# Attention values with weights block-diagonal over two heads, and one more weight unit kept on the chip

## The chip, the cores and the metric

The kernel runs on one core of a Trainium2 chip. A core has five engines that run their own instruction streams: TensorE (PE, matmuls and weight loads), VectorE (DVE), ScalarE (ACT), GpSimd (POOL) and SyncE (SP, which only issues transfers here). SBUF is the on-chip memory of 128 partitions, PSUM the accumulator memory of 128 partitions with eight banks, and 16 DMA engines move data between memory and SBUF. The metric is the time of one execution on the device in microseconds, taken as the median of the runs.

## The reference

The output is the sum of the input, a memory-augmented attention over the normalized input, and a feed-forward block. The attention is a recurrence over 64 segments of 32 tokens: eight memory rows come out of each segment and go into the next.

```python
def _A_ref(x, mem0, Wq, Wk, Wv, Wo, seg_len):       # x (1, 2048, 1024), 32 heads of 128
    mask = (idx[:, None] < M) | (idx[:, None] >= idx[None, :])      # M = 8 memory rows, L = 40
    mem = mem0
    for s in range(n_seg):                                          # 64 segments
        h = jnp.concatenate([mem, x[:, s * seg_len:(s + 1) * seg_len]], axis=1)   # 40 rows
        q, k, v = (einsum('btd,dhe->bhte', h, W) for W in (Wq, Wk, Wv))
        scores = jnp.where(mask, einsum('bhqe,bhke->bhqk', q, k) * scale, -1e9)
        o = einsum('bhqk,bhke->bhqe', softmax(scores), v)
        o = einsum('bhte,hed->btd', o, Wo)
        mem = o[:, :M]
        outs.append(o[:, M:])
    return jnp.concatenate(outs, axis=1)

xn = _layernorm(x)
return x + _A_ref(xn, ...) + (gelu(xn @ w1 + b1) @ w2 + b2)
```

All weights are bfloat16. Wq, Wk, Wv and Wo hold 4 x 8 MB. They don't all fit in SBUF, and every segment needs all of them.

## The kernel before

The feed-forward block and the normalization run first, up to about 370 us. Then comes a loop over the 64 segments. The weights are cut into 64 units of 128 x 2048 elements (512 KB): 16 each of K, Q, V and O, each of K, Q and V in two half passes (u = 0 and 1: heads 0 to 15 and 16 to 31) of eight units. 46 units stay in SBUF. 18 are brought anew in every segment into a ring of six slots; of these one is copied from PSUM, where it is kept in two of eight banks (IN_PSUM), and one (HALF) has half of it in a third bank and the other half in a place of its own in SBUF (half_home), so 16 whole units per segment come from memory.

```python
PLACED = "S....S.." "..S....S" "...S...S" "...S...S" "....S..." ".S.S..S." ".S..S..S" "..S..S.S"   # S: streamed
IN_PSUM = [unit for unit in ORDER if IS_STREAMED[unit]][3]
HALF = [unit for unit in ORDER[48:] if IS_STREAMED[unit]][3]

def start_stream(slot):                    # called whenever a streamed unit has been used
    n = starts.popleft()
    unit, t = streams[n], slab(slot)
    if unit in kept_in:
        for c0, bank in kept_in[unit]:
            nc.vector.tensor_copy(out=t[:, c0:c0 + 1024], in_=bank)        # L228
    elif unit in copies:
        nc.sync.dma_start(out=t[:, :], in_=copies[unit])                   # L230
```

A unit of K, Q or V is four matmuls of 512 columns, side by side in four column groups of TensorE (L690). A segment's last eight rows ("left rows") take part in their segment's attention too, but they are projected for four segments together, in one extra product (psL, hrL) in some of the passes. So the four kinds of segment (i4 = 0 to 3) differ in matmul work.

Attention, per half of the heads. The 16 heads lie as four groups c with four heads j each; the keys of head j of a group are on partitions 32j to 32j+31.

```python
def scores(u):                             # mixed: one PSUM bank
    ...                                    # scores of 40 queries x 4 groups into mixed[:, 0:224]
    pr = pr_last[:, 0:224] if u else sp.tile([P, 256], BF16, name="pr", tag="e")[:, 0:224]
    nc.scalar.activation(out=pr, in_=mixed[:, 0:224], func=ACT.Exp, scale=INV_SQRT_DH)
    ...                                    # masks, by min: L811

def sums(u):
    prA, prB = st["pr", u]
    dA = mixed[:, 0:160].rearrange("p (c q) -> p c q", q=40)
    ...                                    # 4 + 4 matmuls with ones, block by block (bd): L819, L825
    nc.scalar.activation(out=dA, in_=dA, func=ACT.Ln)                      # L829
    nc.scalar.activation(out=dA, in_=dA, func=ACT.Exp, scale=-1.0)         # L830
    nc.vector.tensor_tensor(out=prA, in0=prA, in1=dA, op=ALU.mult)         # L831
    nc.vector.tensor_tensor(out=prB4, in0=prB4, in1=ends(dA), op=ALU.mult) # L833

def values(u, r):                          # two heads b of each group, 32 rows each
    V, (prA, prB) = st["V", u], st["pr", u]
    av = [mixed[:, 256:512] if low_bank and b == 0 else new_acc() for b in range(2)]
    oV = [t[:, 0:160].rearrange("p (c q) -> p c q", q=40) for t in av]
    for c in range(4):
        for b in range(2):
            q = slice(64 * r + 32 * b, 64 * r + 32 * b + 32)
            nc.tensor.matmul(oV[b][:, c, :], lhsT=V[q, c * P:(c + 1) * P], rhs=prA[q, c, :], ...)   # L844
        for b in range(2):
            ...                            # the same with the left rows' values VL: L850
    for b, cp in enumerate((nc.scalar.copy, nc.vector.tensor_copy)):
        hs = slice(8 * r + 4 * b, 8 * r + 4 * b + 4)
        cp(out=outs[u][:, hs, NL * slot:NL * slot + 40], in_=oV[b])        # L857
```

The order in a segment: K0, Q0, K1, Q1, V0, V1, O. scores(0) stands after the first unit of Q1, sums(0) after its last; scores(1) after the first unit of V1, values(0, r) and sums(1) further on in V1, values(1, r) in O. In O the first eight units read d_oL (heads of u = 0) and the last eight b_oL (u = 1), 256 columns a matmul (L870). Three PSUM banks serve as accumulators (acc), one holds scores and sums (mixed), one the masks and the queries of left rows (beside), three the kept weights.

At a segment's end the memory rows go through ACT (L954), TensorE (put_mem, L262) and DVE (L266) into hr, which is the left operand of the next segment's products; the residual is added (L969) and the rows go out.

The softmax here doesn't subtract the row's maximum and nothing guards it: scores larger than these inputs give would overflow.

## Time and profile before

| what | value |
|---|---|
| median of three runs | 1960.52 us (1956.52 to 1964.47) |
| span of the profiled execution | 1969.5 us, TensorE clock 0.981 |
| DMA packets, bytes | 219883, 627.06 MB |
| weight transfers in the loop (u<-Wc) | 1024 of 512 KB |
| TensorE's share of the chain that ended last | 69%; DMA 16%, issue 7% |

How to read the views. The page's first part gives busy time, share and instructions of each engine; "PEld" are weight loads, which overlap matmuls. The DMA row gives the share of the 16 DMA engines in each of 40 equal slices, in tenths. A queue's row gives packets, megabytes and the share of the engines' time. A row of a line gives engine, operation, tile, count, shortest, median and longest duration in ns, first and last start in us, and the shape. A row of stretches gives the stretch, its length, busy time and count of PE, PEld, DVE, ACT and POOL, the granted clock, the DMA share and GB/s. A row of waits gives who waited for what, the sum in us, how often, and the longest. In a timeline a bracket is idle time before the instruction and what ended it; "issue" is idle time that no semaphore in the profile ends. Matmuls are pipelined and their ends are modelled, so a busy TensorE is not TensorE at its peak.

### The profile page before, as it was taken

The numbers are of one execution on the slowest core, as the hardware profiler recorded it, in microseconds if no ns is written. First come the engines' busy times: TensorE is split into PE (matmuls) and PEld (weight loads), VectorE is DVE, ScalarE is ACT, GpSimd is POOL, SyncE is SP. The second block draws the span as 40 slices with busy tenths as digits, with TensorE's granted clock in tenths as the row PEclk, the third lists the DMA queues.
The fourth block names the chain that finished last, engine by engine and source line by source line (L and its number), as shares of the span: only waits on it lengthen the run. The fifth ranks groups of instructions, "written<-read, shape, count | busy, mean of one in ns | idle before, by whom it ended". The sixth has DMA issues, their size and how long they took to land.

```text
span 1969.5 us, 77311 instructions
## 1 busy us (share of the span) xinstructions
PE 1774.1 (90%) x34307; PEld 980.5 (50%) x34307; DVE 886.2 (45%) x2280; ACT 599.5 (30%) x1355; POOL 276.2 (14%) x538
## 2 busy tenths in 40 slices
PE   7999999989888989888989889889888889899887
PEld 3444444445545544455555545455446445545544
DVE  6656565414444444344444444344444444444433
ACT  6343434312223323222222222223222222222222
POOL 0000000002421112121112111111111111111111
PEclk9999999999999999999999999999999999999999
DMA  9821212789999999999999999999999999999998
GB/s 331 252 55 43 55 43 54 283 308 341 381 381 375 388 366 365 354 356 364 378 358 385 370 363 367 363 358 379 359 356 353 380 338 370 383 369 366 367 369 308
DMA packets 219883, 627.06 MB, mean 318 GB/s; under 512 B 47211, under 2 KB 65307, under 8 KB 219548
## 3 DMA queue, kind: packets, MB, share of 16 engines
q1 hardware_dynamic: 199132, 601.96, 82.3%
q0 software_dynamic: 16320, 17.52, 2.7%
q8 instruction: 268, 4.39, 0.9%
q10 hardware_dynamic: 4096, 2.64, 0.4%
q14 instruction: 67, 0.55, 0.1%
HBM read 607.77 MB, written 30.47 MB: 324 GB/s over the span
## 4 chain that ended last, share of the span: by engine, by line
PE 69%; DMA 16%; issue 7%; DVE 4%; ACT 2%; POOL 1%; ACTq 0%; DVEq 0%; POOLq 0%; SPq 0%
PE acc L690 29%; PE acc L870 15%; PE ps L483 10%; DMA u<-Wc_O 8%; PE ps L532 7%; DMA out_dram<-res 4%; PE ps L567 2%; DMA u<-Wc_V 2%; PE mixed L844 2%; DMA u<-Wc_Q 1%; POOL out_dram L1007 1%; PE acc L844 1%; DVE b_oL L748 1%; PE mixed L794 1%; DVE d_oL L899 1%
## 5 line engine op out<-in xcount | busy, mean ns | idle before, releaser
L690 PE MATMUL acc<-u,hr 128*32 128x512 bf16 x11520 | 789.6, 382 | 28.0 <-issue 15.3
L690 PEld LDWEIGHTS <-hr 128*32 128x32 bf16 x12288 | 354.6, 97 | 291.1 <-issue 62.1
L690 PE MATMUL acc<-u,hrL 128*32 128x512 bf16 x2880 | 265.2, 393 | 25.6 <-issue 13.8
L870 PE MATMUL acc<-u,d_oL 128*32 128x256 bf16 (+1 forms) x3552 | 192.6, 297 | 25.5 <-DMA u<-Wc_O 13.9
L483 PE MATMUL ps<-u 128*128 128x512 bf16 x896 | 195.9, 382 | 2.6 <-ACT u L367 2.6
L870 PEld LDWEIGHTS <-b_oL 128*32 128x32 bf16 (+1 forms) x3552 | 117.1, 104 | 81.9 <-issue 48.8
L870 PE MATMUL acc<-u,b_oL 128*32 128x256 bf16 (+1 forms) x1554 | 119.5, 305 | 30.8 <-issue 29.1
L532 PE MATMUL ps<-u 128*128 128x512 bf16 x672 | 147.0, 379 | 0.0
L228 DVE COPY u<-kept 128x1024 bf16<-128x1024 bf16 x190 | 125.0, 686 | 42.4 <-PE acc L690 19.7
L483 PEld LDWEIGHTS <-u 128*128 128x128 bf16 x896 | 88.1, 98 | 109.2 <-issue 4.0
L870 PEld LDWEIGHTS <-d_oL 128*32 128x32 bf16 (+1 forms) x3552 | 103.4, 100 | 69.2 <-issue 44.2
L690 PEld LDWEIGHTS <-hrL 128*32 128x32 bf16 x3072 | 92.9, 98 | 89.8 <-issue 47.8
L266 DVE CAST hr<-mixed 128x64 bf16<-128x64 f32 x63 | 14.1, 224 | 259.1 <-PE mixed L262 249.5
L870 PE MATMUL acc<-W_O,b_oL 128*32 128x256 bf16 (+1 forms) x1776 | 115.5, 307 | 12.9 <-issue 12.9
L748 DVE STREAM_TRANSPOSE b_oL<-b_oL 128x512 bf16<-128x512 bf16 x128 | 90.6, 708 | 61.1 <-ACT b_oL L734 61.1
L844 PEld LDWEIGHTS <-v 32*128 32x128 bf16 x2048 | 64.3, 91 | 101.3 <-issue 70.8
L924 POOL DMA_DIRECT2D res<-hr_d x59 | 33.2, 562 | 537.2 <-PE mixed L825 297.4
L734 ACT CAST kT<-acc 128x512 bf16<-128x512 f32 x64 | 37.4, 585 | 220.0 <-PE acc L690 220.0
L532 PEld LDWEIGHTS <-u 128*128 128x128 bf16 x672 | 65.3, 98 | 77.4 <-DVE g_u L499 0.4
L738 ACT CAST v<-acc 128x512 bf16<-128x512 f32 x128 | 75.3, 589 | 78.4 <-PE acc L690 78.4
L734 ACT CAST b_oL<-acc 128x512 bf16<-128x512 f32 x128 | 75.4, 589 | 76.8 <-PE acc L690 76.8
L1007 POOL DMA_DIRECT2D out_dram<-res x124 | 63.5, 516 | 227.5 <-DVE res L969 226.0
(143 smaller groups left out, 2225.7 us busy)
## 6 DMA issues: line engine op xcount, KB each, us to landing
u<-Wc_O SPq DMA_DIRECT2D x320, 512.0 KB
u<-Wc_K SPq DMA_DIRECT2D x256, 512.0 KB
u<-Wc_V SPq DMA_DIRECT2D x256, 512.0 KB
u<-Wc_Q SPq DMA_DIRECT2D x192, 512.0 KB
u<-in_B_w_dram SPq DMA_DIRECT2D x14, 512.0 KB
u<-in_A_Wq_dram SPq DMA_DIRECT2D x13, 512.0 KB
u<-in_A_Wv_dram SPq DMA_DIRECT2D x12, 512.0 KB
u<-in_A_Wk_dram SPq DMA_DIRECT2D x9, 512.0 KB
```

Source lines behind the costliest of these rows:

```text
L228: nc.vector.tensor_copy(out=t[:, c0:c0 + 1024], in_=bank)
L483: nc.tensor.matmul(ps[:, :].rearrange("p (s t) -> p s t", t=SEG), lhsT=w1_sb[fb // 14 * 8 + kt][:, (fb % 14) * P:(fb % 14 + 1) * P], rhs=x ...
L532: nc.tensor.matmul(ps[:, :], lhsT=gts[fc // 4][:, fc % 4, t * P:(t + 1) * P], rhs=w2_sb[fc // 2][:, fc % 2, cs], start=(fc == 0), stop=(fc ...
L567: nc.tensor.matmul(pss[2 * t + nb][:, :], lhsT=gts[fc // 4][:, fc % 4, t * P:(t + 1) * P], rhs=w2_sb[fc // 2][:, fc % 2, nb * 512:nb * 512 ...
L690: nc.tensor.matmul(o, lhsT=lhs[:, i, :], rhs=m, start=(i == seq[0]), stop=(i == seq[-1]), tile_position=(0, 32 * j),)
L734: cp(out=out, in_=ps.rearrange("p (h e) -> p h e", e=32))
L738: cp(out=t[:, :], in_=ps[:, :])
L748: nc.vector.transpose(out=home, in_=home)
L844: nc.tensor.matmul(oV[b][:, c, :], lhsT=V[q, c * P:(c + 1) * P], rhs=prA[q, c, :], start=(c == 0), stop=False, skip_group_check=True, tile ...
L870: nc.tensor.matmul(acc[r:r + n // 8, 0:n], lhsT=lhs[:, 4 * (i % 4) + 2 * u + k, :], rhs=w_k[:, n * jq:n * jq + n], start=(unit == O_UNITS[ ...
L924: eng.dma_start(out=st["res"][:, :], in_=hr_d[s + 1, :, 256:512])
L1007: nc.gpsimd.dma_start(out=out_flat[rows, 256 * j:256 * j + 256], in_=res[32 * j:32 * j + NX, :])
```

## The change

It does three things.

First, values takes two heads b of a group in one matmul. The probabilities, divided by their sums, are laid out block-diagonally: for rows of head b = 0 the 40 columns of b = 1 are zero, and the other way round. So one matmul of 64 rows and 80 columns stands for two of 32 rows and 40 columns. The zeros come from the exponential: exp(-ln(sum) + off), where off is 0 for the rows of the block and -30000 for the others.

Second, the masks and the kept queries of left rows move out of a PSUM bank of their own into the free end of the bank of the scores, as bfloat16 bits. That frees a bank.

Third, the freed bank takes a fourth half of weights: a whole second unit (IN_BANKS, the last streamed one of O) is copied from PSUM, and half_home serves another unit of O (HALF), whose other half is streamed. So 15 whole units and one half come from memory in each segment.

```diff
-SCRATCH = 512
-SMALL = 3584
+SCRATCH = 352
+SMALL = 3744
+AT_BANKS, AT_HALF = 5, 2
-HALF = [unit for unit in ORDER[48:] if IS_STREAMED[unit]][3]
+STREAMED_O = [unit for unit in ORDER[48:] if IS_STREAMED[unit]]
+IN_BANKS, HALF = STREAMED_O[AT_BANKS], STREAMED_O[AT_HALF]
+KEPT = (IN_PSUM, IN_BANKS)
@@ start_stream
+        elif unit == HALF:
+            nc.sync.dma_start(out=t[:, 1024:2048], in_=copies[unit])
@@ banks
-        beside = banks.tile([P, 512], F32, name="beside")
-        qS = beside[:, 0:48 * NL].rearrange("p (i h t) -> p i h t", i=3, h=16)
-        kept = banks.tile([P, 3, 1024], BF16, name="kept")
+        there = mixed[:, 340:512].bitcast(BF16)
+        qS = there[:, 0:32 * NL].rearrange("p (i h t) -> p i h t", i=2, h=16)
+        kept = banks.tile([P, 4, 1024], BF16, name="kept")
@@ scores
-                pr = pr_last[:, 0:224] if u else sp.tile([P, 256], BF16, name="pr", tag="e")[:, 0:224]
+                pr = pr_all[:, 0:224]
@@ sums
-                        dA[q, :, :], lhsT=bd[:, q], rhs=prA, ...
+                        dA[q, :, :], lhsT=bd[:, j:j + 1].to_broadcast([P, 32]), rhs=prA, ...
-                nc.scalar.activation(out=dA, in_=dA, func=ACT.Ln)
-                nc.scalar.activation(out=dA, in_=dA, func=ACT.Exp, scale=-1.0)
-                nc.vector.tensor_tensor(out=prA, in0=prA, in1=dA, op=ALU.mult)
-                nc.vector.tensor_tensor(out=prB4, in0=prB4, in1=ends(dA), op=ALU.mult)
+                nc.scalar.activation(out=mixed[:, 0:160], in_=mixed[:, 0:160], func=ACT.Ln)
+                for b in (1, 0):
+                    nc.scalar.activation(
+                        out=mixed[:, 160 * b:160 * b + 160], in_=mixed[:, 0:160], func=ACT.Exp, scale=-1.0,
+                        bias=off[:, b:b + 1],
+                    )
+                nc.vector.tensor_tensor(out=pdA..., in0=prA[:, None, :, :].to_broadcast([P, 2, 4, 40]), in1=dd, op=ALU.mult)
+                nc.vector.tensor_tensor(out=pdB..., in0=prB..., in1=dd..., op=ALU.mult)
@@ values(u, rs)
+                av = {r: new_acc() for r in rs}
+                    for r in rs:
+                        q = slice(64 * r, 64 * r + 64)
+                        nc.tensor.matmul(oV[r][:, c, :, :], lhsT=V[q, c * P:(c + 1) * P], rhs=pdA[q, c, :, :], ...)
+                for r in rs:
+                    cp = nc.vector.tensor_copy if r else nc.scalar.copy
+                    cp(out=out.rearrange("p (b c) q -> p c b q", b=2), in_=oV[r])
@@ places in the passes: V1, then O
-            at = {0: [lambda: scores(1)], 2: [lambda: values(0, 0)], 4: [lambda: values(0, 1)], 6: [lambda: sums(1)]}
-            at[5] = [load_res]
+            at = {0: [lambda: scores(1)], 4: [lambda: sums(1)]}
+            if left_v[1]:
+                at.update({1: [lambda: values(0, (0,))], 3: [lambda: values(0, (1,))]})
+            else:
+                at[1] = [lambda: values(0, (0, 1))]
-            at = {4: [lambda: values(1, 0)], 6: [lambda: values(1, 1)]}
+            if left_v[1]:
+                at = {4: [lambda: values(1, (0,))], 6: [lambda: values(1, (1,))]}
+            else:
+                at = {5: [lambda: values(1, (0, 1))]}
+            at.setdefault(0, []).append(load_res)
@@ the residual's tile, and the rows of the next segment
-                st["res"] = sp.tile([P, 256], BF16, name="res", tag="e")
+                st["res"] = pr_all
-        hr = hrp.tile([P, 256], BF16, name="hr")
+        eng.dma_start(out=hr_home[:, :], in_=hr_d[s, :, 0:256])
... (the rest: tile places, keep(IN_BANKS, ...) in the first segment, one output transfer cut in two)
```

Two kinds of order change with it. In V1, values(0) comes after unit 1 instead of units 2 and 4, and sums(1) after unit 4 instead of 6. In O, values(1) comes after unit 5 instead of 4 and 6, except in the segments with left values in V1 (left_v[1], one of four), where the accumulators suffice for one r at a time. The load of the residual moves from V1 to the first unit of O.

## The prediction

> **What bounds the kernel now.** I read the page first, then the busy time by stretches, the idle time of TensorE by releaser, the timeline of TensorE, and last the rows of the lines that change.
>
> ```profile
> PE 1774.1 (90%) x34307; PEld 980.5 (50%) x34307; DVE 886.2 (45%) x2280; ACT 599.5 (30%) x1355; POOL 276.2 (14%) x538
> DMA  9821212789999999999999999999999999999998
> q8 instruction: 268, 4.39, 0.9%
> L266 DVE CAST hr<-mixed x63: 223/224/226, 465.3 to 1942.4; 128x64 bf16<-128x64 f32 x63
> 465.30:1942.40 1477.10, 1309.99 (x31236) 763.25 (x31225) 624.78 (x1622) 419.46 (x1054) 259.70 (x485) 0.98 0.98 368
> ```
>
> L266 runs once per segment, so 62 segments take 1477.1 us: 23.82 us each. In them TensorE is busy 89%, and the 16 DMA engines 98% (last but one column) at 368 GB/s. Two resources are nearly full, and the question is which one the other waits for. The idle time of TensorE from 500 to 1900 us (58.8 segments) says it:
>
> ```profile
> PE acc L870 <- issue: 51.4, 35, 2.8
> PE acc L690 <- issue: 37.5, 34, 2.5
> PE acc L870 <- DMA u<-Wc_O: 14.4, 29, 1.5
> PE acc L690 <- DVE kL L734: 8.6, 15, 0.8
> PE acc L844 <- issue: 8.2, 8, 1.9
> ```
>
> All rows ending in "issue" add up to 113 us in 119 stops (1.93 us a segment); all rows that wait for a weight transfer to 22.5 us (0.38 a segment); ACT and DVE to 18 us (0.30). So TensorE seldom waits for weights. What "issue" is, the timeline shows:
>
> ```profile
> 1077.55 0.27 PE L870 MATMUL acc<-u,b_oL 128*32 128x256 bf16 x1 [1.03 <-issue]
> ...
> 1095.16 0.39 PE L690 MATMUL acc<-u,hrL 128*32 128x512 bf16 x1 [0.94 <-issue]
> ...
> 1100.56 0.18 PE L850 MATMUL acc<-pr_last,VL 32*128 32x16 bf16 x1 [1.09 <-issue]
> ```
>
> These stops fall inside a unit, at instructions with no semaphore to wait for, and from one to the next the trace has 384 and 128 matmuls: multiples of 128. A matmul comes with a weight load, so that is 256 instructions; and (34307 + 34307) / 268 packets of the instruction queue is 256. TensorE stops because its next 256 instructions have not arrived. They come over the DMA engines that the weights keep 98% busy.
>
> **What the Trainium skill says.** "Runtime: NRT & Kernel Launch", Instruction fetch mechanics: instructions are refilled in 16 KiB blocks of 256 over a DMA queue of the sequencer's own, and the cost is "mostly hidden". The trace agrees on the blocks (4.39 MB in 268 packets) and not on the cost: 1.93 us of 23.82. "DMA: Bandwidth & Descriptors", Issuing engines are not separate DMA queues: all queues share the 16 engines. It agrees: a 64 KB load of GpSimd's queue (hr) takes 5.6 us to land. "TensorE: Matmul & The Clock Gate", LDWEIGHTS: the load's time goes by the columns, not the rows. So 64-row value weights should load as 32-row ones do (91 ns here); no row of this trace has 64. "VectorE: DVE Perf Modes", perf-mode tier table: a tensor_tensor with a PSUM operand goes at the slowest rate. L831 and L833 below agree: 96 elements more cost 106 to 108 ns.
>
> **The change part by part**, per segment, averaged over the four kinds of segment.
>
> ```profile
> L844 PE MATMUL acc<-pr_last,v x704: 173/174/212, 459.9 to 1959.7; 32*128 32x40 bf16 x176
> L831 DVE TENSOR_TENSOR pr_last<-pr_last,mixed x64: 320/321/323, 459.2 to 1956.2; 128x160 bf16<-128x160 bf16 x64
> L833 DVE TENSOR_TENSOR pr_last<-pr_last,mixed x64: 211/214/217, 459.5 to 1956.5; 128x64 bf16<-128x64 bf16 x64
> L829 ACT ACTIVATE mixed<-mixed x128: 288/288/288, 448.7 to 1955.6; 128x160 f32<-128x160 f32 x128
> L857 ACT CAST b_oL<-acc x48: 292/292/293, 483.3 to 1958.7; 128x160 bf16<-128x160 f32 x48
> L228 DVE COPY u<-kept x190: 678/684/693, 460.2 to 1955.4; 128x1024 bf16<-128x1024 bf16 x190
> ```
>
> *Value matmuls.* 64 become 32. In the trace a call of values (16 matmuls) takes 0.29 us from its first start to the next product's, and 0.10 us before it beyond the usual spacing: 0.39 us, four calls, 1.55 us. In three segments of four the change makes two calls of them, 16 matmuls each in pairs. Four sums matmuls of 160 columns take 0.07 us, 0.44 ns a column, so a pair of 80 takes 0.035 us; one of 32 stays at the 0.024 us of today's pairs: 4 x 0.059 + 0.19 = 0.43 us a call, 0.86 in all, 0.69 saved. In the fourth kind four calls stay, and get 0.04 dearer each: -0.16. Mean: 0.48 us saved.
>
> *Instructions.* 32 matmuls and 32 weight loads fewer. A segment has 1012 TensorE instructions on average, 3.95 blocks of 256; it will have 948, 3.70 blocks.
>
> *Weight transfers.* 16 units of 512 KB become 15.5: 256 KB at 368 GB/s is 0.71 us of the DMA engines' time.
>
> *Longer chains.* sums gains an exponential on ACT (0.29 us), and the multiplications grow from 320 + 212 to about 500 + 285 ns (estimates from L831 and L833: 1.1 ns an element). For u=1 that lies between the sums, now at unit 4 of V1, and values(1) at O unit 5: 1.95 us of matmuls against about 2.0 us of chain, 0.1 us of wait. For u=0 the extra exponential stands before the cast of q on ACT and the multiplications before its transpose on DVE: near 1068 us scores(1) already waited about a quarter of a microsecond for that transpose. It comes 0.5 us later, which I expect to be felt in two of four segments: +0.25. values(1) now ends two units (0.43 us) before O unit 8 reads b_oL, which an ACT copy of 320 elements (427 ns, from 292 for 160 and 589 for 512) must have written: +0.25 in two of four, +0.12.
>
> *One more unit from PSUM.* Two DVE copies instead of one, 0.69 us each. They may start when unit 55 frees its slot, and unit 63 needs both: 1.37 us plus waking up, against seven units of 0.215 us = 1.5. About +0.2. DVE itself, 42% busy, has room.
>
> *First segment.* One more piece is turned into PSUM; the third took 2.5 us here (435.8 to 438.3). +2.5 us once.
>
> **The sum.** Without instruction waits a segment takes 23.82 - 1.93 = 21.89 us. Add -0.48 + 0.25 + 0.10 + 0.12 + 0.20, and -0.15 for fewer waits on weights: 21.93 us. Per block that is 5.54 us now and 5.93 after. A block that arrives late is less late when there is 0.39 us more work before it is wanted. About half of the blocks are late today (119 stops, 233 blocks), and fewer will be; at 0.42 of them on average the wait shrinks by 0.16 from 0.49 to 0.33 us a block: 1.22 us a segment. So 23.15 us, 0.67 less. By 62 segments that is 41.5 us, less 2.5: 1960.5 - 39 = 1921 us.
>
> Can the DMA engines follow? 0.98 x 23.82 - 0.71 = 22.6 us of work in 23.15 us is 98% again: yes, barely.
>
> **The rivals.** (a) DMA alone sets the pace. For it: 98% busy. Against it: 0.38 us of weight waits a segment, and segments differ with their matmul work at equal bytes. It gives 0.71 x 62 = 44 us less, near 1917: almost the same time by another way. (b) Instruction blocks alone set the pace, 6.03 us each whatever the work: 3.70 x 6.03 = 22.3 us, held up by the DMA's 22.6: 60 to 75 us less, near 1892. For it: half of the blocks are late. Against it: the other half are not. (c) New waits eat the gain. The sums of both halves, the copies from PSUM and the residual row all moved closer to their users; the residual's load, which began right after the sums at unit 6 of V1, waits for the multiplications now (2.0 us after the sums at unit 4), so it starts about 1.4 us later, while it takes 5.7 us to land and the addition holds one of three accumulators. If the waits come to 1.3 us instead of 0.67, a segment loses only 0.25 us: 1947. (d) The bytes saved are hidden and the instructions are few: 1955.
>
> **Range and chances.** My sum, (a) and (b) point below or at the 2% line (1921.3), (c) and (d) above it; (c) is as likely as (b). So 1921 us, 1892 to 1952, faster by 2% with 0.48, within 2% with 0.47, slower with 0.05.
>
> **What would show it.** Right: 252 packets in the instruction queue (64,552 TensorE instructions in the changed program, 68,616 before); "issue" rows of TensorE near 75 us where they were 113; a segment near 23.15 us; DMA share still 0.97 to 0.98; in the waits, DVE rows before scores(1) and before the last O unit that grew. If the stops are as many and as long as before but the segment shorter by 0.7 us, (a) was right. If waits on b_oL, on u copied from kept, or DVE's wait for the residual come to over a microsecond a segment, (c) was. If DMA's share falls to 0.95 with the time unchanged, TensorE's own waits rule and I mis-sized them.

## The result: slower, by 1.3%

The changed kernel takes 1987.86 us (median of 4 runs, 1985.70 to 1990.74); the kernel before, run beside it, 1962.49. The ratio is 1.0129 with an interval of 1.0092 to 1.0166. Predicted were 1921 us, and 1892 to 1952 as the range: a miss in size and in sign. The interval leaves out 1, so the loss is clear of the noise, small as it is.

The page of the changed kernel has these lines in place of the first three shown of before:

```profile
PE 1747.1 (88%) x32275; PEld 938.2 (47%) x32275; DVE 918.9 (46%) x2222; ACT 638.5 (32%) x1356; POOL 286.6 (14%) x554
DMA  9821212888889999999999999999999999899997
q8 instruction: 253, 4.15, 0.8%
```

The parts that were to shrink did: 253 instruction packets where there were 268, and 27 us less of busy TensorE. Yet TensorE is busy for a smaller share, and the DMA row has eights from the tenth slice to the twelfth where before it had nines. The stretch of the loop from the first copy of hr to the last:

```profile
468.10:1957.70 1489.60, 1283.92 (x29252) 720.53 (x29244) 655.94 (x1560) 456.64 (x1054) 269.42 (x500) 0.98 0.95 353
```

The DMA engines fell from 98% to 95% busy, from 368 to 353 GB/s, while the loop grew from 1477.1 to 1489.6 us. Neither of the two full resources is fuller; something else holds them both. The waits of TensorE from 500 to 1900 us (who waits for what, sum in us, times, longest):

```profile
PE acc L902 <- DMA u<-Wc_O: 36.5, 54, 2.6
PE mixed L836 <- DVE pr_all L828: 30.2, 21, 7.3
PE acc L709 <- DVE hr_home L281: 18.6, 13, 3.2
PE mixed L811 <- DVE b_oL L767: 17.4, 27, 0.8
PE acc L709 <- issue: 15.4, 21, 1.9
PE acc L709 <- DVE pd_main L1012: 15.1, 12, 2.2
PE acc L902 <- issue: 11.0, 12, 2.3
PE mixed L811 <- DVE mixed L640: 9.8, 15, 0.7
```

All rows ending in "issue" make 33 us, where they made 113. All rows that wait for a weight transfer make 42.5 us (before 22.5). What grew are the rows that wait for DVE and ACT: 108 us, before 18. Four places lead them: the softmax's sums (L836, 30 us, which wait for the masked probabilities), the scores (L811, 27 us in two rows), the addition of the residual, after which the accumulator is free (L1012, 19 us in two rows, of which the larger is shown), and the memory rows copied into the next segment's rows (L281, 19 us).

When does the time go? The starts of the copy of hr, once a segment, give it:

| us | segments 1 to 10, in all | later ones, each |
|---|---|---|
| before | 233.1 | 23.92 |
| changed | 257.0 | 23.71 |

So the change loses 24 us in ten segments and wins back 11 in the other 52. These are one traced execution each, and that of the kernel before was a long one (1971.2 us, its median 1962.5); the later segments of kernels much like it, below, take 23.7 to 23.9 us. So the 24 us stand firmer than the 11. The first ten show what went wrong. This is the timeline of the fourth, thinned out (start, duration, engine, line, operation; in brackets the idle time before and what ended it):

```profile
550.45 0.43 DVE L1012 TENSOR_TENSOR pr_all<-acc,pr_all 128x256 bf16<-128x256 f32 x1 [2.08 <-DMA pr_all<-hr_d]
550.87 0.55 POOL L446 DMA_DIRECT2D hr_d<-R_n  x1 [4.69 <-issue]
...
556.29 1.12 POOL L1051 DMA_DIRECT2D out_dram<-pr_all  x2 [2.68 <-issue]
...
563.83 0.36 ACT L823 ACTIVATE pr_all<-mixed 128x224 bf16<-128x224 f32 x1 [8.25 <-DMA out_dram<-pr_all]
564.58 0.33 PE L836 MATMUL mixed<-pr_all,small_consts 128*32 128x160 bf16 x4 [7.30 <-DVE pr_all L828]
```

Read it from the end. TensorE stands for 7.3 us at the sums. They need the probabilities in pr_all, which ACT couldn't write for 8.25 us, because the transfer of the previous segment's output still read pr_all: one tile serves both. That output was complete at 550.88, but GpSimd began its transfer at 556.29 only. In between GpSimd issued older transfers of its queue, copies of normalized rows (hr_d<-R_n and hrL_d<-R_n, 57 of them between 471 and 574 us), and before several of them it stood for 3 to 5 us, waiting for nothing that the profile shows ("issue"). The largest rows of such stops of GpSimd in the loop are, with one row of the kernel before as the last,

```profile
POOL out_dram L1048 <- issue: 91.8, 16, 7.0
...
POOL hr_d L446 <- issue: 28.9, 12, 4.8
...
POOL hr_d L431 <- issue: 21.9, 9, 5.4
```

The first row, the second half of the output transfer that the change cut in two, has no counterpart before; the second has the last. In the first ten segments all such stops of GpSimd come to 49 us, before to 23. A later segment shows what that first row does:

```profile
1012.51 0.67 POOL L1048 DMA_DIRECT2D out_dram<-outM_d  x1 [4.65 <-DMA outM_d<-pr_all]
1018.61 0.63 POOL L1048 DMA_DIRECT2D out_dram<-outM_d  x1 [5.44 <-issue]
1024.29 0.60 POOL L254 DMA_DIRECT2D hr_home<-hr_d  x1 [5.05 <-PE acc L882]
```

The second half waits 5.4 us for nothing named. The landings in the trace tell for what: each of the 16 stops of the first row above ends 0.3 us after the first half has landed. The next segment's rows follow 5.7 us later again. Their row names L882, but that line doesn't read hr_home: it is merely the event that came last. The last products that read hr_home start at 1021.12 in the trace and last 0.4 us, so the tile was free some 2.8 us before the load was issued; and in all 14 cases in which this load stops behind the second half, it is issued 0.3 us after that half has landed. On average over the segments of that kind (i4 = 3, from the eleventh) the load of the next rows is issued 3.0 us before the end of O, where it was 6.3; the residual's, over all later segments, 4.1 us before it where it was 7.7. The Trainium skill, "DMA: Bandwidth & Descriptors", section SWDGE vs HWDGE vs iDMA, says that GpSimd writes the descriptors of its transfers itself, into rings in a part of SBUF. SCRATCH is that part here (the kernel sets dynamic_dma_scratch_size to it), and the change took it from 512 to 352 bytes per partition to make room. The traces agree that it bounds the transfers in flight: where only copies of normalized rows are under way, never more than 5 of them are issued and not yet landed in the changed kernel, and up to 8 in the kernel before. That is theory D below; the expectations call SCRATCH the ring.

### The profile page after: what moved, and what is told of

It is laid out like the page before. It is cut to its first block, busy times and chain, and to the rows that moved or that the text cites. A ratio compares the mean times of both kernels' runs of the same rounds, so it can differ in the third digit from the quotient of the medians.

```text
span 1986.2 us, 73232 instructions
## 1 busy us (share of the span) xinstructions
PE 1747.1 (88%) x32275; PEld 938.2 (47%) x32275; DVE 918.9 (46%) x2222; ACT 638.5 (32%) x1356; POOL 286.6 (14%) x554
## 5 line engine op out<-in xcount | busy, mean ns | idle before, releaser
L709 PE MATMUL acc<-u,hr_home 128*32 128x512 bf16 x11520 | 791.8, 387 | 60.7 <-DVE hr_home L281 21.3
L709 PEld LDWEIGHTS <-hr_home 128*32 128x32 bf16 x12288 | 345.6, 98 | 360.3 <-issue 62.4
L902 PE MATMUL acc<-u,d_oL 128*32 128x256 bf16 (+1 forms) x3330 | 173.2, 290 | 18.8 <-DMA u<-Wc_O 15.9
L242 DVE COPY u<-kept 128x1024 bf16<-128x1024 bf16 x254 | 163.0, 683 | 16.0 <-PE acc L902 7.2
L857 DVE TENSOR_TENSOR pd_main<-pr_all,mixed 128x320 bf16<-128x320 bf16 x128 | 61.9, 484 | 143.6 <-ACT mixed L850 141.5
L709 PEld LDWEIGHTS <-hrL 128*32 128x32 bf16 x3072 | 85.4, 97 | 86.5 <-issue 24.5
L828 DVE TENSOR_TENSOR pr_all<-pr_all,mixed 128x96 bf16<-128x96 bf16 (+1 forms) x256 | 37.9, 189 | 166.1 <-ACT pr_all L823 166.1
L902 PE MATMUL acc<-W_O,b_oL 128*32 128x256 bf16 (+1 forms) x1776 | 106.2, 289 | 6.1 <-issue 6.1
L254 POOL DMA_DIRECT2D hr_home<-hr_d x58 | 33.1, 571 | 488.8 <-PE acc L709 394.0
L281 DVE CAST hr_home<-mixed 128x64 bf16<-128x64 f32 x63 | 14.1, 225 | 186.6 <-PE mixed L277 120.1
L997 ACT CAST d_oL<-acc 128x256 bf16<-128x256 f32 (+1 forms) x63 | 26.8, 426 | 221.3 <-PE acc L902 221.3
```

The costliest lines, as they stand in the source:

```text
L254: eng.dma_start(out=hr_home[:, :], in_=hr_d[s, :, 0:256])
L281: nc.vector.tensor_copy(out=hT[:, :, NX:SEG].rearrange("p (j c) t -> p j c t", c=nc_), in_=psM.rearrange("p c j t -> p j c t"),)
L709: nc.tensor.matmul(o, lhsT=lhs[:, i, :], rhs=m, start=(i == seq[0]), stop=(i == seq[-1]), tile_position=(0, 32 * j),)
L828: nc.vector.tensor_tensor(out=p, in0=p, in1=m[:, None, :].to_broadcast([P, 4, n]), op=ALU.min)
L857: nc.vector.tensor_tensor(out=pdA.rearrange("p c b q -> p b c q"), in0=prA[:, None, :, :].to_broadcast([P, 2, 4, 40]), in1=dd, op=ALU.mult,)
L902: nc.tensor.matmul(acc[r:r + n // 8, 0:n], lhsT=lhs[:, 4 * (i % 4) + 2 * u + k, :], rhs=w_k[:, n * jq:n * jq + n], start=(unit == O_UNITS[ ...
```

## The experiments

Every ratio is against the kernel before, run beside it on the same chip. All kernels in one table first; the last two columns are read as in the table above, from one traced execution each. The kernel before had medians of 1962.5 to 1969.6 us beside the groups, so differences in us between runs of different groups are good to some microseconds only.

| kernel | us | ratio [interval] | segments 1 to 10 | later, each |
|---|---|---|---|---|
| changed | 1987.9 | 1.0129 [1.0092, 1.0166] | 257.0 | 23.71 |
| a_nores | 1937.5 | 0.9845 [0.9804, 0.9886] | 246.7 | 23.02 |
| a_res | 1952.9 | 0.9915 [0.9884, 0.9945] | 245.3 | 23.25 |
| a_res_hr | 1939.1 | 0.9868 [0.9815, 0.9920] | 245.0 | 22.94 |
| b_late | 1961.7 | 0.9977 [0.9957, 0.9996] | 235.6 | 23.68 |
| a_dge | 1927.1 | 0.9807 [0.9744, 0.9870] | 230.0 | 23.04 |
| a_res_dge | 1919.9 | 0.9764 [0.9706, 0.9821] | 234.4 | 22.83 |
| a_16_all | 1915.9 | 0.9749 [0.9690, 0.9807] | 234.0 | 22.75 |
| b_fewer | 1913.9 | 0.9728 [0.9679, 0.9777] | 233.3 | 22.88 |
| b_split | 1966.6 | 1.0003 [0.9981, 1.0024] | 236.4 | 23.84 |
| b_ring | 1994.2 | 1.0126 [1.0086, 1.0165] | 256.9 | 23.82 |
| a_16_res_dge | 1913.2 | 0.9721 [0.9678, 0.9763] | 232.3 | 22.88 |
| a_16_sum | 1901.9 | 0.9657 [0.9608, 0.9706] | 228.5 | 22.54 |
| a_dge_cut | 1933.4 | 0.9849 [0.9793, 0.9905] | 234.6 | 23.02 |
| a_dge_ring | 1982.1 | 1.0067 [1.0034, 1.0100] | 257.7 | 23.66 |
| b_ring_late | 1999.2 | 1.0183 [1.0123, 1.0242] | 259.2 | 24.02 |

**First group: the residual's load.** The first theory (L) was rival (c) of the prediction: the residual is loaded later, into pr_all, and TensorE ends up waiting for it. In a_nores the load is left out, and with it the addition of input and feed-forward block for a segment's own rows; the output lacks that part.

```diff
--- changed
+++ a_nores
-                eng.dma_start(out=st["res"][:, :], in_=hr_d[s + 1, :, 256:512])
... (the rest: a copy in place of the addition)
```

> The changed kernel without the transfer of the residual of the segment's own rows: the output product is copied into the row tile instead of being added to it (the rows go out without input and feed-forward; the left rows keep their addition). Theory L (late loads: the residual arrives 1 us or more after the end of O, and the addition, the accumulator and the next probabilities wait for it): 15 to 40 us less than the changed kernel, 1950 to 1972 us; DVE's copy at the end of a segment starts within 0.3 us of the copy into hr_home in all segments but those that wait for hr_home. Theory S (the longer sums chain and the second copy from PSUM cost it): within 8 us of the changed kernel, 1980 to 1992 us.

It is 50 us below the changed kernel, more than theory L named. This proves less than it seems: without the load, GpSimd's queue is shorter too, and pr_all no longer takes a transfer between the probabilities and the output. The first ten segments, at 246.7 us, stay 14 us above before.

a_res gives the residual a tile of its own and its old early place; the SBUF for it comes from keeping 512 columns of a unit instead of 1024.

```diff
--- changed
+++ a_res
-                st["res"] = pr_all
+                st["res"] = spare[:, 0:256]
+            at[5] = [load_res]              # at unit 5 of V1, as in the kernel before
-            at.setdefault(0, []).append(load_res)
... (the rest: half_home of 512 columns, and spare beside it)
```

> The changed kernel with a tile of its own for the residual, loaded at unit 5 of V1 as before. The 512 bytes come from half_home, which keeps 512 columns of the HALF unit instead of 1024, so 15.75 units are streamed instead of 15.5. Theory L: 15 to 35 us less than the changed kernel (1953 to 1973 us), the addition within 0.5 us of the copy into hr_home on average. Theory S: no gain, and 0.35 us a segment more for the quarter unit: 1985 to 2010 us.

a_res_hr has a second tile for the next rows as well, so that they are loaded before V0.

```diff
--- a_res
+++ a_res_hr
-        eng.dma_start(out=hr_home[:, :], in_=hr_d[s, :, 0:256])
+        home = spare[:, 256:512] if s % 2 else hr_home[:, :]
+        eng.dma_start(out=home, in_=hr_d[s, :, 0:256])
... (the rest: load_x_rows called before V0)
```

> As a_res, and two tiles for the rows of the next segment in turns, loaded before V0 instead of after V1. Theory L, with the second late load (hr_home, on average 0.4 us later after O than before, 1.4 us in the segments with left values in V1): another 10 to 30 us less than a_res, 1930 to 1955 us, and no row of waits of hr_home for its transfer. Theory S: same as a_res.

Both win, 35 and 49 us on the changed kernel, and in both the first ten segments still cost 12 us more than before. b_late is the test from the other side, the kernel before with nothing but a late load:

```diff
--- before
+++ b_late
-            at[5] = [load_res]              # at unit 5 of V1
+            at.setdefault(5, []).append(load_res)     # at unit 5 of O
```

> The kernel before with one edit: the load of the residual moved from unit 5 of V1 to unit 5 of O, which puts its issue about 4 us before the end of O as in the changed kernel. Theory L: 15 to 40 us slower than the kernel before, 1975 to 2000 us, with the extra time above all in the first ten segments. Theory S: within 6 us of the kernel before.

It isn't slower at all. Theory L as stated falls: a load as late as this costs nothing by itself. (The test is weaker than meant: its load is issued 6.0 us before the end of O on average, in the changed kernel 4.1.)

**Second group: GpSimd's descriptors, and the bytes.** a_dge is the changed kernel with SCRATCH at 512 and the output transfer in one piece. The room again comes from keeping 512 columns in place of 1024, so it moves 128 KB more per segment. The residual stays late and in pr_all.

```diff
--- changed
+++ a_dge
-SCRATCH = 352
-SMALL = 3744
+SCRATCH = 512
+SMALL = 3584
-    half_home = nc.alloc_sbuf_tensor_at("half_home", [P, DM], BF16, offset=SCRATCH)
+    half_home = nc.alloc_sbuf_tensor_at("half_home", [P, 512], BF16, offset=SCRATCH)
-                for t in (slice(0, NX // 2), slice(NX // 2, NX)):
-                    small.append(lambda o=o[:, t, :], r=r[:, t, :]: nc.gpsimd.dma_start(out=o, in_=r))
+                small.append(lambda o=o, r=r: nc.gpsimd.dma_start(out=o, in_=r))
... (the rest: places of the other tiles)
```

> The changed kernel with GpSimd's descriptor ring as before the change (512 bytes instead of 352) and the output of the third kind of segment in one transfer again; the residual stays late. The bytes come from half_home, which keeps 512 columns, so 15.75 units are streamed. Theory D (the smaller ring makes GpSimd's queue stop, for 3 to 7 us at a time, above all in the first ten segments, in which the feed-forward rows are copied): first ten segments 257 us to about 245, GpSimd's issue waits (above 140 us on the changed kernel) to under 40 us, in all 10 to 25 us less than the changed kernel: 1963 to 1978 us. Without D: 1985 to 2000 us.

61 us less than the changed kernel, although more bytes move. Theory D named 10 to 25: it had counted on the first ten segments only (here 230.0 us of 257.0), and each later one became shorter too, 23.04 us of 23.71. a_res_dge joins this with a_res:

```diff
--- a_dge
+++ a_res_dge
-                st["res"] = pr_all
+                st["res"] = spare[:, 0:256]     # and loaded at unit 5 of V1
```

> As a_dge, and a tile of its own for the residual, loaded at unit 5 of V1. Theories L and D together: 10 to 20 us less than a_res (1953 us): 1930 to 1943 us, the first ten segments within 4 us of the kernel before. Without D: 1950 to 1960 us.

a_16_all keeps no part of HALF, so all 16 units come from memory, and uses the room for both tiles:

```diff
--- a_res_dge
+++ a_16_all
-        elif unit == HALF:
-            nc.sync.dma_start(out=t[:, 512:2048], in_=copies[unit])
+        home = spare[:, 256:512] if s % 2 else hr_home[:, :]
+        eng.dma_start(out=home, in_=hr_d[s, :, 0:256])
... (the rest: half_home given up, load_x_rows called before V0)
```

> Sixteen whole units streamed as before the change (HALF comes whole, half_home is given up), and the 2 KB used for all that became scarce: the residual's tile, two tiles for the next rows, the ring of 512 bytes. So of the change the value matmuls stay, and the whole unit in PSUM. If the bytes of weights count (a quarter unit is 0.35 us a segment of the DMA engines): 1945 to 1965 us, 0.3 us a segment more than a_res_dge. If instruction supply and matmuls count and bytes hardly: 1925 to 1940 us.

a_res_dge and a_16_all came out some 10 us below the ranges named for them. The four kernels a_dge, a_res_dge, a_16_all and a_16_res_dge (below) lie within 14 us of each other, and their intervals overlap: with SCRATCH at 512 the place of the residual makes 7 us between a_dge and a_res_dge, which is within the noise, and the bytes make nothing that these runs show. a_16_res_dge asks the latter cleanly, with the residual's tile and no second tile for the rows:

```diff
--- a_res_dge
+++ a_16_res_dge
-        elif unit == HALF:
-            nc.sync.dma_start(out=t[:, 512:2048], in_=copies[unit])
... (the rest: half_home given up)
```

> All 16 units of O from DRAM (no part kept in SBUF), residual in a tile of its own, ring of 512 bytes, one outM transfer: beside a_res_dge (1919.9 us), which keeps a quarter of a unit and so moves 131 KB less per segment, and a_16_all (1915.9), which loads the next rows earlier in a second tile. Theory W (the streamed weights' bytes are hidden once the queue is not empty): within 8 us of a_res_dge, 1912 to 1928. Rival B (DMA at 95% of the time is the bound, 131 KB at 368 GB/s are 0.36 us a segment and 22 us in all): 1935 to 1950.

1913 against 1920 us, with more bytes. So a quarter of a unit in SBUF brings nothing that these runs can see. The half unit of the change was not tried with SCRATCH at 512: the changed kernel's tiles fill all that 352 bytes leave.

**Third group: TensorE's instructions.** b_fewer is the kernel before without the left rows' value matmuls: 64 TensorE instructions fewer per segment, as in the change, and nothing moved. The work of these matmuls goes with them. The output lacks the part of the left rows.

```diff
--- before
+++ b_fewer
-                    for b in range(2):
-                        q = slice(64 * r + 32 * b, 64 * r + 32 * b + 32)
-                        nc.tensor.matmul(ends(oV[b])[:, c, :, :], lhsT=VL[u][q, c * P:(c + 1) * P], ...)
```

> The kernel before without the matmuls of the left rows' values (L850; the output lacks their part): 32 matmuls and 32 weight loads fewer in each segment, as many instructions as the change takes away, nothing else moved. Theory F (TensorE waits for its instructions): the issue waits of TensorE from 500 to 1900 us fall from 113 to 85 us or less, and the time by 25 to 45 us, of which the matmuls themselves are about 0.1 us a call, 25 us. If the DMA engines alone set the pace: less than 8 us.

2.7% faster, 54 us or 0.87 us a segment, more than the 25 to 45 named. Its stretch of the loop, and its waits of TensorE, 500 to 1900 us:

```profile
463.70:1886.90 1423.20, 1279.51 (x29252) 713.64 (x29244) 622.93 (x1623) 419.56 (x1054) 260.34 (x485) 0.99 1.00 381
...
PE acc L863 <- DMA u<-Wc_O: 34.8, 60, 1.8
PE acc L863 <- issue: 31.0, 24, 2.3
PE acc L690 <- issue: 22.2, 32, 2.0
```

The "issue" rows together fell from 113 to 65 us, and the waits for weights rose from 22.5 to 48: a TensorE that loses less time to its instructions seems to run ahead and wait for weights now and then. The net is what counts. The loop is 54 us shorter than before (1423.2 us for 1477.1), and TensorE's busy time 30 us (1279.5 for 1310.0): about half of that is the work of the matmuls left out, the other half is less time at half clock, as the last section shows. So by this estimate some 15 of the 54 us are the matmuls' own work; the rest, 24 us of fewer waits and 15 of clock, can come from fewer instructions.

**Fourth group: SCRATCH alone, in the kernel before.** A pair. b_split cuts the output transfer in two; b_ring does the same and sets SCRATCH to 352. They differ in nothing else.

```diff
--- before
+++ b_split
-                small.append(lambda o=o, r=r: nc.gpsimd.dma_start(out=o, in_=r))
+                for t in (slice(0, NX // 2), slice(NX // 2, NX)):
+                    small.append(lambda o=o[:, t, :], r=r[:, t, :]: nc.gpsimd.dma_start(out=o, in_=r))
```

> The kernel before, with nothing but the output transfer outM -> out_dram cut in two, ring of 512 bytes as before. Theory D (the loss of the change comes from GpSimd's ring of 352 bytes, not from the cut that it forced): within 8 us of the kernel before, 1955 to 1970 us; GpSimd's waits of the kind 'out_dram <- issue' stay under 25 us in the whole run. Rival (the second half of the cut transfer, not the ring, holds up GpSimd's queue): 1985 to 2020 us, and some 90 us of such waits, as in the changed kernel.

```diff
--- b_split
+++ b_ring
-SCRATCH = 512
-SMALL = 3584
+SCRATCH = 352
+SMALL = 3744
```

> The same kernel as b_split with the ring cut from 512 to 352 bytes and nothing else, so that it lies beside b_split as a test of the ring alone in a kernel without the change's other parts. Theory D: 1990 to 2025 us (25 to 60 us over b_split), with 90 us or more of GpSimd's issue waits, and most of the loss in the first ten segments, where the copies of R are made. Rival T (the ring hurts only together with the shared tiles of the changed kernel: probabilities, residual): within 10 us of b_split. Rival B (bytes or instructions alone decide): the same as b_split, since neither changes.

b_split is as fast as before, b_ring 28 us slower: intervals of 0.9981 to 1.0024 and 1.0086 to 1.0165. (SCRATCH at 352 also moves the small tiles by 160 bytes; that this is the cause wasn't tested apart, but the stops' ends at landings speak for the room.) GpSimd's stops in b_ring, whole run:

```profile
POOL out_dram L1005 <- issue: 35.1, 6, 6.6
POOL hr_d L431 <- issue: 31.1, 11, 4.7
POOL pr_last L949 <- issue: 9.6, 2, 4.9
```

In b_split the second is 18.6 us and the others aren't there. Copies of normalized rows in flight are at most 5 in b_ring and up to 8 in b_split. The loss lies in the first ten segments: 20.5 us (256.9 against 236.4) of 21.7 between the two traced executions, and to the microsecond the first ten of the changed kernel. All of GpSimd's stops from the first copy of hr on are 95 us, in b_split 22. But those at the cut transfer, 35 us, are far fewer than the 92 of the changed kernel, and they cost nothing in the later segments.

**Fifth group: the later segments.** Between the changed kernel and a_dge lie 0.67 us in each later segment, 35 us in all, which b_ring doesn't have. a_dge_cut and a_dge_ring split it: a_dge with the transfer cut again, and then with SCRATCH at 352.

```diff
--- a_dge
+++ a_dge_cut
-                small.append(lambda o=o, r=r: nc.gpsimd.dma_start(out=o, in_=r))
+                for t in (slice(0, NX // 2), slice(NX // 2, NX)):
+                    small.append(lambda o=o[:, t, :], r=r[:, t, :]: nc.gpsimd.dma_start(out=o, in_=r))
```

> a_dge (1927.1 us; the changed kernel with a ring of 512 bytes and a quarter of a unit kept in SBUF) with the output transfer outM -> out_dram cut in two again. Theory D (the ring's size alone): within 8 us of a_dge, 1919 to 1935 us, and under 15 us of GpSimd's issue waits at that transfer. Rival T (the second half of the cut transfer holds up GpSimd's queue, where the probabilities' tile waits for the outputs): 1950 to 1990 us.

```diff
--- a_dge_cut
+++ a_dge_ring
-SCRATCH = 512
-SMALL = 3584
+SCRATCH = 352
+SMALL = 3744
```

> a_dge_cut with the ring at 352 bytes and nothing else: the ring alone, beside the changed kernel's instructions and shared tiles. Theory D: 1970 to 1995 us, 45 us or more over a_dge_cut: some 24 us of it in the first ten segments, the rest in the later ones (23.0 to 23.6 us a segment), because here the output transfers that the ring delays keep the tile of the probabilities. Rival H (the ring costs only in the first ten segments, as in b_ring, and the later loss of the changed kernel comes from the half unit kept in SBUF or its load): 1945 to 1958 us, later segments as in a_dge at 23.0.

The cut costs nothing that can be told, SCRATCH 49 us by the medians: 1933.4 (1925 to 1941) and 1982.1 (1966 to 2001), ratios 0.9849 and 1.0067 with intervals far apart. Of the 56 us between their loops 23 lie in the first ten segments and 33 in the later ones (0.63 us each); the loop of a_dge_cut starts 5 us later, which makes up the difference. The timeline of GpSimd in a_dge_cut, in the same stage of a group of four segments as the one shown of the changed kernel (L1053 is L1048 there, L257 is L254):

```profile
993.21 1.32 POOL L1053 DMA_DIRECT2D out_dram<-outM_d  x2 [5.50 <-DMA outM_d<-pr_all]
1001.94 0.59 POOL L257 DMA_DIRECT2D hr_home<-hr_d  x1 [7.41 <-PE acc L715]
```

Both halves go out one behind the other ("x2"), and the load of the next rows waits for nothing but L715, the product that reads their tile. In a_dge_ring the second half is held again: its row is 89.2 us in 16 stops. TensorE's waits in a_dge_cut, 500 to 1900 us, show what SCRATCH did to them (the same three were 30.2, 18.6 and, with the row of pd_main, 19.1 us in the changed kernel):

```profile
PE mixed L842 <- DVE pr_all L834: 22.9, 18, 2.5
...
PE acc L715 <- DVE hr_home L284: 3.1, 4, 2.1
PE acc L715 <- DVE pr_all L1017: 2.9, 3, 1.7
```

b_ring_late, b_ring with the late residual of b_late, asks why b_ring pays nothing later:

```diff
--- b_ring
+++ b_ring_late
-            at[5] = [load_res]
+            at.setdefault(5, []).append(load_res)
```

> b_ring (1994.2 us: the kernel before with the ring of 352 bytes and the cut transfer) with the residual loaded late, at unit 5 of O, as in b_late. Theory J (ring and late residual work together: a transfer of the residual that starts late into a blocked queue comes after the addition): 2005 to 2025 us, with later segments above b_ring's 23.8 us. Rival S (they are separate, and a late residual costs nothing without a tile shared with the probabilities): 1985 to 2003.

The stops at the cut transfer are back, 80.4 us in 14, and a later segment takes 24.02 us against 23.82 in b_ring and 23.68 in b_late. But 1999 us lies below what theory J named and within what S named, and the intervals of b_ring and b_ring_late overlap: that the late residual is what makes room scarce in the later segments fits the stops, and is not shown by the time.

**A version that beats both.** a_16_sum is a_16_all with the softmax's sums by one full matrix of ones in blocks of 32: two matmuls in place of eight in each half.

```diff
--- a_16_all
+++ a_16_sum
-                for j in range(4):                         # and the same for prB
-                    nc.tensor.matmul(dA[q, :, :], lhsT=bd[:, j:j + 1].to_broadcast([P, 32]), rhs=prA,
-                                     start=True, stop=False, tile_position=(0, 32 * j))
+                nc.tensor.matmul(dA[:, :, :], lhsT=bd[:, :], rhs=prA, start=True, stop=False)
```

> The best version so far (a_16_all, 1915.9 us) with the softmax's sums by one 128 x 128 matrix of ones in blocks: 2 matmuls in place of 8 in each half, so 12 TensorE instructions fewer per half and 24 fewer per segment. Theory F (TensorE's instructions are worth their place in the supply, 54 us for 64 per segment in b_fewer): 20 us less, 1890 to 1905 us, TensorE's issue waits below those of a_16_all. Rival S (the sums lie on the chain between the exponential and the logarithm, and four 32-column matmuls run beside each other in the array while one full one does not): 1910 to 1930 us. In no case more than 1935.

1901.9 us, ratio to before 0.9657: the fastest of all. It is 14 us below a_16_all, whose interval just touches its own, so the gain of this last step is likely rather than certain. If it is one, it comes from fewer waits: TensorE is busy for longer (1011.6 us from 700 to 1800 us, 990.9 in a_16_all), while its "issue" rows fall from 49 to 28 us.

## Why the prediction was wrong

By its own steps:

- *What bounds the kernel now*: the stops at instruction blocks were there, 113 us, in 96 stops and not the 119 that the prediction counts (so 41% of the 233 blocks were late, not half). They were the largest wait of TensorE, but not all of them could be won, because other waits took their place.
- *Instructions*: 3.70 blocks were predicted for 3.95, 253 packets came of 268. "1.22 us a segment" of stops was too high: 33 us over the 58.3 segments from 500 to 1900 us are 0.57. The term of -0.71 measured -1.36.
- *Weight transfers*: "-0.15 for fewer waits on weights" had the wrong sign. They went from 0.38 to 0.73 us a segment (42.5 / 58.3), in b_fewer and a_dge_cut (44 us) likewise. It looks as if two kinds of lateness lay one over the other, and taking one away uncovers part of the other. And of the 256 KB saved the half that was tried is worth nothing visible (a_16_res_dge).
- *Value matmuls*: -0.48 is borne out in size. TensorE's busy time in the loop fell from 1310.0 us to 1283.9, 0.42 a segment, and to 1271.0 in a_dge_cut, 0.63; with the time at half clock counted half, 0.32 and 0.37.
- *Longer chains*: for scores(1) 0.25 us were predicted; the rows of L811 come to 27.2 us, 0.47 a segment, 0.05 before. For b_oL 0.12 were predicted, and no row waits for it; for the u=1 sums 0.10, and L876 waits for "issue" only. For *one more unit from PSUM* 0.20: 4.5 us wait for a copy of L242, 0.08. These four, 0.67 together, measured about 0.5. But the sums of both halves, whose chain became longer as well, wait most of all (L836), in a_dge_cut too, and all waits for DVE and ACT are 1.15 us a segment there, 0.85 more than before. The durations behind the four hold, in the lines of the changed kernel (median in ns between the slashes):

```profile
L876 PE MATMUL acc<-pd_main,v x1024: 192/193/244, 456.0 to 1976.1; 64*128 64x80 bf16 x171
L876 PEld LDWEIGHTS <-v x1024: 91/93/141, 456.0 to 1976.0; 64*128 64x128 bf16 x171
L857 DVE TENSOR_TENSOR pd_main<-pr_all,mixed x128: 448/489/490, 449.8 to 1973.8; 128x320 bf16<-128x320 bf16 x128
L861 DVE TENSOR_TENSOR pd_left<-pr_all,mixed x128: 273/280/283, 450.2 to 1974.2; 128x128 bf16<-128x128 bf16 x128
L890 ACT CAST b_oL<-acc x64: 425/425/426, 461.4 to 1976.3; 128x320 bf16<-128x320 f32 x64
```

  The estimates were 500, 285 and 427 ns, and 91 for the load of 64 rows.
- *First segment*: +2.5 predicted, +2.8 measured (first copy of hr at 468.1 instead of 465.3), which is luck: the kernels without the additional piece have this copy at 460.8 to 465.3, those with it at 467.2 to 473.3.
- *The signs on record*: the packets came as named (252, measured 253); but DMA's share fell to 0.95, and the waits for DVE and ACT came to 1.85 us a segment, over the microsecond set for (c).
- *Rival (c)* was nearest: "New waits eat the gain" names the residual as loaded "about 1.4 us later". It is 3.6 us later (4.1 before the end of O, not 7.7), and the addition comes 1.1 us later on average.

**The step that failed is the list itself**: the change part by part has no term for SCRATCH 512 to 352, though the diff begins with it, and (c) counts for the residual's delay only the longer chain ahead of it, not the queue that it lies in. The runs put the missing term at 28 us in the kernel before (b_ring against b_split) and 49 us in the changed one (a_dge_ring against a_dge_cut). With the old SCRATCH, and a quarter of a unit kept in place of the half, the changed kernel gives 1933 us in a_dge_cut and 1927 in a_dge, within the range on record. So about the expected gain did come: the later segments of a_dge_cut take 23.02 us (predicted 23.15), and SCRATCH gave it back, about 1.4 times over by the ratios.

That the total fits so well is partly luck. The loop of a_dge_cut:

```profile
472.80:1904.60 1431.80, 1270.96 (x29252) 717.34 (x29244) 657.77 (x1560) 456.97 (x1054) 269.92 (x500) 0.99 0.99 373
```

It is 0.73 us a segment shorter than before. By terms: TensorE's busy time -0.63 (predicted -0.48), stops at instruction blocks -1.30 (-0.71), waits for weights +0.34 (-0.15), waits for DVE and ACT +0.85 (+0.67). Of the 45 us, 39 are busy time (about 16 of them less time at half clock) and 6 are waits: what fewer stops for instructions saved in waits, the other waits took back almost whole.

Open remains whether the half unit in SBUF adds a few microseconds more: the changed kernel is 6 us above a_dge_ring, and their intervals overlap.

## What to carry to other kernels

When a change frees a few hundred bytes, ask whose they were: the room that an engine has for transfers in flight is a resource like a PSUM bank, and cutting it stopped the whole in-order queue behind it here, loads and outputs alike. Look for it in the waits of that engine that end in "issue", at the busiest stage, not in the average, and see whether they end at a landing. Then ask what stands behind them: a_res_dge has 86.5 us of such stops with SCRATCH at 512, before the residual's load, and is among the fastest; there this load is issued 11.9 us before the end of O, in the changed kernel 4.1. And when a change takes one wait away, expect the others to grow: here TensorE's stops for instructions fell by 75 us between 500 and 1900 us in a_dge_cut, and its other waits rose by 74.

## What the runs showed of the hardware

A long stop costs more than its length. The stretches around the stop of 7.3 us at the sums, in the changed kernel (the last three columns are granted clock, DMA share and GB/s):

```profile
558.00:562.00 4.00, 0.00 (x0) 0.00 (x0) 0.00 (x0) 0.00 (x0) 1.29 (x3) 0.98 1.02 400
...
564.00:566.00 2.00, 1.03 (x16) 0.41 (x20) 1.75 (x5) 1.07 (x4) 2.00 (x4) 0.50 0.20 35
566.00:568.00 2.00, 2.00 (x24) 0.75 (x20) 1.75 (x5) 0.66 (x2) 1.74 (x4) 0.50 0.18 43
568.00:570.00 2.00, 2.00 (x40) 0.83 (x36) 0.00 (x0) 0.00 (x0) 2.00 (x5) 0.84 0.11 17
```

TensorE comes back at half its clock, and has the whole of it only about 4 us after work began again (the half lasts from 561.8 to 568.6). The Trainium skill, "TensorE: Matmul & The Clock Gate", section What's actually happening, gives at least one idle window of about 3.4 us for the fall to half and one busy window for the return; this stop of 7.3 us fits both. Meanwhile all slots of the weights fill, and the DMA engines fall to 11% to 20% busy for 6 us: time that the busiest resource of this kernel doesn't get back. Over the first ten segments the granted clock averages 0.95 in the changed kernel and 0.99 in the kernel before. TensorE is 6 to 7 us longer busy there for the same instructions (213.6 us in a_dge_ring against 207.3 in a_dge_cut, 218.1 in b_ring against 210.9 in b_split): a third or so of the 20 to 23 us lost there.

Shorter stops do it too. In the kernel before, a stop of 2.05 us for instructions ended at 817.47; the stretches are the 3.41 us around it, the next and the one after:

```profile
817.47 0.40 PE L870 MATMUL acc<-W_O,b_oL 128*32 128x256 bf16 x8 [2.05 <-issue]
...
815.03:818.44 3.41, 1.36 (x44) 0.76 (x32) 0.00 (x0) 0.30 (x1) 0.00 (x0) 1.00 0.89 334
818.44:821.85 3.41, 3.41 (x48) 1.49 (x44) 1.70 (x4) 0.07 (x1) 1.94 (x4) 0.50 1.00 360
821.85:825.26 3.41, 3.41 (x72) 1.66 (x68) 0.93 (x3) 1.17 (x2) 0.10 (x1) 1.00 0.67 237
```

TensorE was busy for 40% of the first stretch, and the second went at half clock: here the window was not idle as a whole. The loop of this kernel has 18 such stretches of 3.4 us, and 17 of them lie at a stop for instructions of 1.2 to 2.8 us (though not every stop of that length brings one). TensorE is busy for 60 of these 61 us, so some 30 us are lost there, an estimate; in b_fewer and a_dge_cut such stretches are down to 29 us. This is part of what a stop for instructions costs, and the prediction, which counts only the stops' length, has no term for it.

A matrix's columns don't set the time of its load here, other than the section LDWEIGHTS that the prediction drew on has it: the sums' loads of 32 columns take 97 ns (median, changed kernel), the ones of 128 columns in a_16_sum 95 and 98. That 64 rows load as fast as 32 did come out (93 and 91 ns).
